# Zero-weight spare matmuls, a finer-grained head and a per-tile last layer norm in a two-layer attention kernel

## The chip, the cores and the metric

The kernel runs on one core of a Trainium2 chip. The metric is device time in microseconds (us). "The kernel before" is the tuned kernel that the change starts from, "the changed kernel" is the one after it. A run is called fast or slow by its state, and has the mean granted clock of the matrix engine beside it, where 1.0 is full speed. A single execution of this kernel varies with that clock by several us (the kernel before beside bz_late: 1630.98 us at 0.986, 1637.15 at 0.978), so every comparison below is made with several runs, and traces are compared by where in them a difference arises.

The engines: PE multiplies matrices (PEld is its weight load), ACT computes activation functions, DVE is the vector engine, POOL the general one, SP issues transfers.

## The reference

Two identical layers of attention and a GELU network on 2048 tokens of 512 values, with 32 heads of 16 values each:

```python
x = A_x                                                       # 1 x 2048 x 512, bf16
x = x + _A_ref(_layernorm(x), A_wqkv, A_wo)                   # attention, 32 heads
x = x + _B_ref(_layernorm(x), B_w1, B_b1, B_w2, B_b2)         # 512 -> 1792 -> 512, GELU
x = x + _A_ref(_layernorm(x), A_wqkv, A_wo)
x = x + _B_ref(_layernorm(x), B_w1, B_b1, B_w2, B_b2)
# _A_ref: softmax(q k^T / 4) v per head, then times wo
```

The softmax has 2 x 32 x 2048 x 2048 exponentials. They are cut into cells of 128 keys by 512 queries: 4096 cells, each one score matmul on PE.

## The kernel before

The program is laid out at build time by a scheduler that simulates the engines: generators yield operations with an estimated cost, a priority and the buffers that they read and write, and for each engine the scheduler picks the next one. Any edit that changes an operation's cost, priority or place can rearrange everything that comes after it.

Most cells go to ACT, as one instruction for one to three cells; the rest go to DVE, which makes an exponential with integer arithmetic in three steps.

```python
# ACT, in exps(): n cells of scores from PSUM to a buffer of probabilities
yield _Op("act", 0.065 + 0.4267 * n, lambda e, src=src, dst=dst: e.activation(
    out=dst, in_=src, func=ACT.Exp, scale=0.25), ...)
...
# DVE: dfirst() reads the scores, dchain() works on 16-bit integers in SBUF
yield _Op("dve", 0.68, lambda e: e.tensor_scalar(u, self.bank(b), E_SCALE, E_BIAS, op0=ALU.mult, op1=ALU.add), ...)
yield _Op("dve", 0.08 + 0.14 * n, lambda e: e.tensor_scalar(U[:, 1, 0:n, :], U[:, 0, 0:n, :], SHIFT, None, op0=ALU.add), ...)
yield _Op("dve", 0.08 + 0.28 * n, lambda e: e.tensor_scalar(U[:, 2:4, 0:n, :], U[:, 0:2, 0:n, :], 2 * SHIFT, None, op0=ALU.add), ...)
```

PE has less to do than ACT (in the trace before it is busy for 1430.3 us, ACT for 1560.7), and after it has idled its clock is at times halved (in the trace before, PE is busy for 0.12 us of the microsecond from 515 us, and the windows after it read 0.50). So the scheduler already puts spare matmuls, whose result nobody reads, into PE's gaps. They go into a PSUM bank that happens to be free, and only where the recent activity in its model is below a threshold:

```python
def fill(self, start, nxt):                       # before PE's next operation nxt, which can start at start
    while self.filler and self.mode:
        ...
        b, t = self.free(now, nxt.writes)         # a bank whose last result has been read
        now = max(now, t)
        if start - now < into + MM + back + FMARGIN or self.active(start) >= WARM:
            return
        op = self.filler(b, mode)                 # W2 times W2, one matmul of 128 columns or four of 32
```

The head: x comes in four transfers of 512 KB, the first tiles are normalized as a block of four, transposed on PE, and projected.

In the middle, once the first chunk's attention is through, POOL writes the ones column of the second layer's V:

```python
yield ("need", ("otn", 0, (0, 0, 512), 3))
yield _Op("pool", 1.0, lambda e: e.memset(T["V"][1][:, :, :, 16:17], 1.0), ...)
```

The tail, after the last exponential, is the output projection of attention (`wo`), a residual add, the last layer norm, the first GELU layer (`hpair`), GELU and the output tiles (`ytile`) of the last 256 tokens.

The softmax here doesn't subtract the row's maximum and nothing guards it: scores larger than these inputs give would overflow.

Of the kernel before, what the change touches and what calls it, by code (L numbers as in the profile page):

```python
# [15 lines left out]
F = 1792  # L16
# [38 lines left out]
WINDOW = 3.4  # L55
WARM = 0.38
FMARGIN = -0.1
FOLD = 0.1
DPRIO = 9
# [146 lines left out]
class _Sched:  # L206
# [5 lines left out]
    def __init__(self, P):  # L212
        self.P = P
        self.clock = {e: 0.0 for e in P.ENGS}
        self.end = {}
        self.pools = {}
        self.tokens = {}
        self.threads = []
        self.nseq = 0
        self.mode = None  # L220
        self.ops = []
        self.stream = []
        self.filler, self.free, self.fills = None, None, set()
# [86 lines left out]
    def fill(self, start, nxt):  # L310
        while self.filler and self.mode:
            now = self.clock["pe"]
            mode = "F" if nxt.mode == self.mode == "F" else "P"
            into, back = SW * (mode != self.mode), SW * (mode != nxt.mode) - SW * (nxt.mode != self.mode)
            b, t = self.free(now, nxt.writes)
            now = max(now, t)
            if start - now < into + MM + back + FMARGIN or self.active(start) >= WARM:
                return
            op = self.filler(b, mode)
            self.mode = mode  # L320
            ev = self.P.group("pe", op.fns, op.reads, op.writes)
            self.fills.add(ev)
            self.note(now + into, now + into + MM, op)
            self.ops.append(("pe", now, into + MM, "FILL"))
            self.clock["pe"] = now + into + MM
            self.end[ev] = self.clock["pe"] + LATENCY["pe"]
# [64 lines left out]
def bass_interleave_layers__mha_block__dense_activation_gelu__prompt_kernel(  # L391
# [15 lines left out]
    with ExitStack() as es:  # L407
# [39 lines left out]
        T["ONES1"] = sb([1, 128], BF16, "ones1")  # L447
        T["IDENT"] = sb([128, 128], BF16, "ident")
# [8 lines left out]
        sem_names = ["pe", "act", "dve", "pool", "dx0", "dx1", "dx2", "dx3", "dwq", "dwk", "dwv", "db1", "db2", "dw2",  # L457
# [37 lines left out]
class _Plan:  # L495
# [8 lines left out]
    def init(self):  # L504
        T, hbm = self.T, self.hbm

        def load(dst, src, sem, keys, cost):
            return _Op("sp", cost, lambda e: e.dma_start(dst, src), writes=keys, sem=sem, by=16, tail=2.0)

        yield _Op("pool", 0.1, lambda e: e.memset(T["IDENT"][:], 0.0), writes=["IDENT"])  # L510
        yield _Op("pool", 0.3, lambda e: e.affine_select(
            out=T["IDENT"][:], in_=T["IDENT"][:], compare_op=ALU.not_equal, fill=1.0, base=0, pattern=[[-1, 128]],
            channel_multiplier=1), reads=["IDENT"], writes=["IDENT"])
        yield _Op("pool", 0.1, lambda e: e.memset(T["NHALF"][:], -0.5), writes=["NHALF"])
        yield _Op("pool", 0.1, lambda e: e.memset(T["ONES1"][:], 1.0), writes=["ONES1"])
        yield _Op("dve", 0.6, lambda e: e.memset(self.bank(PVB), 0.0), writes=["B.%d" % PVB])
        yield _Op("dve", 0.1, lambda e: e.tensor_reduce(
            out=T["MASK"][:, :], in_=T["IDENT"][:, :].rearrange("p (a t d) -> p t a d", a=4, t=2, d=DH),
            axis=mybir.AxisListType.XY, op=ALU.add), reads=["IDENT"], writes=["MASK"])
        yield _Op("pool", 1.0, lambda e: e.memset(T["V"][0][:, :, :, 16:17], 1.0), writes=["V01"])  # L520
        yield ("need", ("otn", 0, (0, 0, 512), 3))
        yield _Op("pool", 1.0, lambda e: e.memset(T["V"][1][:, :, :, 16:17], 1.0),
                  writes=["V11"] + ["PART.0.%d" % g for g in range(8)])
        yield ("give", "v1ones")

    def loads(self):
# [13 lines left out]
        yield lx(0)  # L540
# [17 lines left out]
    def ln(self, tiles, dst, dkeys, prio, quick=False):  # L558
# [13 lines left out]
        yield _Op("pool", 1.0, lambda e: e.tensor_tensor(  # L572
# [8 lines left out]
    def ln_tile(self, c, t, dst, dkeys, quick):  # L581
# [16 lines left out]
        yield _Op("pe", 4 * TR, fns, reads=["XLN.%d" % x, "IDENT"], writes=["B.%d" % b])  # L598
        yield ("rel", "xln", x)
        t3 = tb[:, 0:512].rearrange("p (c q) -> p c q", c=NDC)  # L600
        if ph:
# [6 lines left out]
    def proj(self, l, kind, i, c, src, skeys, ph, done):  # L608
# [34 lines left out]
        if l:  # L643
            for r, j in zip(us, (0, 1) if kind == "V" else (i // 2,)):
                yield from self.wdone((l, (c, 0, 512), kind, j), r)
        cols = slice(512 * c, 512 * (c + 1))
# [9 lines left out]
        elif kind == "Q":  # L656
            yield _Op(ev, DV, lambda e: copy(e, T["Q"][:, i, cols], pb), reads=["B.%d" % b],
                      writes=["Q.%d.%d" % (i, c)])
        else:
            yield _Op("dve", DV, lambda e: e.tensor_copy(T["V"][l][:, i, :, 0:16], pb.rearrange("p (h d) -> p h d", h=H)),  # L660
                      reads=["B.%d" % b],
                      writes=["V%d.%d" % (l, i)] + (["PART.0.%d" % g for g in range(8)] if l else []))
        yield ("rel", "misc", b)
# [30 lines left out]
    def norm(self, l, seg, g, b, part, final):  # L694
# [8 lines left out]
        else:  # L703
            pt, pk = T["PART1"][:, g, :], "PART1.%d" % g
            over = ["K0.%d.%d" % (g // 2, c) for c in range(self.NQ)]
        if not final:
# [135 lines left out]
    def gelu(self, l, seg):  # L842
# [7 lines left out]
        fns = []  # L850
        for f in range(0, NFC, NFC // GP):
            g = T["G"][:, f:f + NFC // GP, seg[1]:seg[1] + n]
            if n == 512:
                g = g.rearrange("p a q -> p (a q)")
            fns.append(lambda e, g=g: e.activation(out=g, in_=g, func=ACT.Gelu_apprx_tanh))  # L855
        gk = self.gkeys(seg, range(NFC))
        yield _Op("act", GP * (0.065 + 0.4267 * NFC / GP * n / 512) + (2 - tail) * 1.28, fns, reads=gk, writes=gk, prio=2)
        for p in range(NFC // 2):
            yield ("give", ("g", l, seg, p))
# [26 lines left out]

    def post(self, l, seg):
# [5 lines left out]
        order = [(i, x) for i in range(NL) for x in self.segs[i]]  # L893
        prev = order[order.index((l, seg)) - 1] if (l, seg) != order[0] else None
# [4 lines left out]
        for t in tiles:  # L899
            yield ("need", ("xready", t, 2 * l + 1))  # L900
        self.phase[c] = 2 * l + 1
# [3 lines left out]
        yield ("spawn", self.ln(tiles, xf, xk, LNP, last), LNP)  # L905
# [31 lines left out]
    def first(self, c):  # L937
        T = self.T
        self.phase[c] = 0
        for t in range(4 * c, 4 * c + 4):  # L940
            yield ("give", ("xready", t, 0))
        yield from self.ln(range(4 * c, 4 * c + 4), lambda t: T["K"][1][:, :, t * 128:(t + 1) * 128], lambda t: ["XL.%d" % t],
                           5 + c, c == 0)
# [34 lines left out]
    def setup_attention(self):  # L978
# [22 lines left out]
        self.ended = False  # L1001
# [17 lines left out]
    def qpad(self):  # L1019
        T = self.T  # L1020
        for pi, (l, seg, g, kts, part, final) in enumerate(self.pas):
            b, ts = self.heads(seg, g)
# [10 lines left out]
    def free(self, now, ahead):  # L1033
        P = self.P
        best = (None, 1e9)
        for b in (6, 7, 0, 1, 2, 3, 4, 5) if "W2" in P.lastw else ():
            k = "B.%d" % b
            if k in ahead or not P.reads.get(k) and P.lastw.get(k) not in self.s.fills:
                continue
            t = max([0.0] + [self.s.end.get(ev, 0.0) + FOLD for ev in P.deps(["W2"], [k]) if ev[0] != "pe"])  # L1040
            if max(t, now) < max(best[1], now):
                best = (b, t)
        return best

    def filler(self, b, mode):
        T = self.T
        fns = []
        for a in range(1 if mode == "F" else 4):
            m = 128 if mode == "F" else 32
            o = self.bank(b)[m * a:m * a + m, :]  # L1050
            fns.append(lambda e, o=o, a=a, m=m: e.matmul(o, lhsT=T["W2"][:, 0, m * a:m * a + m], rhs=T["W2"][:, 1, :], start=True,  # L1051
                                                         stop=True, tile_position=(0, m * a)))
        return _Op("pe", MM, fns, reads=["W2"], writes=["B.%d" % b], mode=mode)
# [322 lines left out]
    def pvs(self):  # L1376
        T = self.T
        pools = self.s.pools
        for pi, (l, seg, g, kts, part, final) in enumerate(self.pas):
# [21 lines left out]
            def build(op, start, pi=pi, b=b, l=l, cols=cols, begun=begun, n=n):  # L1401
# [28 lines left out]
                op.cost = MM * rounds  # L1430

# [83 lines left out]
```

## Time and profile before

| kernel before | value |
|---|---|
| median of all its runs beside the changed kernel | 1632.34 us (1630.91 to 1634.13, 6 runs) |
| profiled span, mean clock | 1629.9 us, 0.986 |
| first exponential starts | 19.52 us |
| middle (first to last exponential) | 1581.28 us: ACT busy 1545.93, idle 35.35 |
| tail (from the last exponential) | 29.10 us |
| stretches at half clock in the middle | 11, together 44.4 us |

The lines themselves stand in the prediction below. They are read as a sum: head, ACT's work, ACT's idle, tail. A change can shorten the time only through one of these four.

### The profile page before, as it was taken

What the parts mean: (1) busy time and instruction counts of PE and PEld (TensorE: products, weight loads), DVE (VectorE), ACT (ScalarE), POOL (GpSimd) and SP (SyncE); (2) the same over time, 40 slices, a digit from 0 to 9 for tenths busy, and PEclk for the clock granted to TensorE, in tenths of its full rate; (3) what the DMA queues carried; (4) which work ended last, traced back from release to release, by engine and by line L of the source; (5) the groups of instructions that cost most, each with busy time, mean ns of one, the idle gap of its engine ahead of it and who ended that gap; (6) DMA issues with size and microseconds to landing.
All of it is one profiled execution on the core that took longest, in us unless ns stands there. A gap on an engine that the chain in (4) does not pass through costs nothing.

```text
span 1629.9 us, 32720 instructions
## 1 busy us (share of the span) xinstructions
PE 1430.3 (88%) x13701; PEld 418.1 (26%) x13838; DVE 1355.2 (83%) x2612; ACT 1560.7 (96%) x1402; POOL 111.6 (7%) x143
## 2 busy tenths in 40 slices
PE   6997888989898989899889989788898889888988
PEld 2222222222222222222222222222222222233434
DVE  6579999878887988987787788888888988897883
ACT  5999999999999999999998999989999999999995
POOL 3200000000000000000110001111000000000000
PEclk9999999999999999999999999999999999999999
DMA  5100001001010011100111001001101100010110
GB/s 173 22 1 1 1 14 34 27 4 39 25 33 27 1 27 40 34 27 1 27 46 47 7 14 40 2 1 27 46 11 30 34 14 11 17 40 24 50 53 27
DMA packets 88319, 44.85 MB, mean 28 GB/s; under 512 B 33645, under 2 KB 88174, under 8 KB 88174
## 3 DMA queue, kind: packets, MB, share of 16 engines
q1 hardware_dynamic: 88174, 42.75, 9.8%
q8 instruction: 111, 1.82, 0.5%
q14 instruction: 34, 0.28, 0.1%
HBM read 33.03 MB, written 2.10 MB: 22 GB/s over the span
## 4 chain that ended last, share of the span: by engine, by line
ACT 58%; PE 36%; DVE 3%; issue 1%; DMA 1%; POOL 0%; ACTq 0%
ACT pt L1360 49%; PE ps L1064 11%; PE ps L1421 11%; PE ps L868 4%; ACT v L1360 4%; PE ps L822 4%; PE ps L638 3%; ACT g L855 3%; ACT kt L1360 2%; PE ps L635 1%; DVE du L1209 1%; PE ps L749 1%; PE ps L1051 1%; ACT L855 1%; DMA xf<-xln 1%
## 5 line engine op out<-in xcount | busy, mean ns | idle before, releaser
L1360 ACT ACTIVATE pt<-ps 128x1024 bf16<-128x1024 f32 (+1 forms) x1217 | 1335.7, 1244 | 30.2 <-PE ps L1064 14.4
L1064 PE MATMUL ps<-qp,kt 32*128 32x512 bf16 x4096 | 545.5, 387 | 149.6 <-ACT pt L1360 109.5
L1209 DVE TENSOR_SCALAR du<-ps 128x512 uint16<-128x512 f32 x650 | 440.1, 685 | 112.7 <-PE ps L1064 106.2
L1421 PE MATMUL ps<-pt,v 128*17 128x512 bf16 (+1 forms) x3205 | 450.9, 364 | 2.3 <-ACT pt L1360 1.0
L1064 PEld LDWEIGHTS ps<-qp,kt 32*128 32x128 bf16 x4096 | 141.9, 91 | 700.6 <-ACT pt L1360 304.1
L1421 PE MATMUL ps<-du,vc 128*17 128x512 bf16 (+1 forms) x2178 | 305.1, 360 | 1.6 <-DVE du L1272 1.1
L1272 DVE TENSOR_SCALAR du<-du 128x2048 uint16<-128x2048 uint16 (+1 forms) x329 | 222.4, 681 | 2.5
L1028 POOL TENSOR_SCALAR qp<-q,mask 128x512 bf16<-128x512 bf16 (+1 forms) x92 | 68.7, 747 | 1273.0 <-PE ps L1064 1263.7
L1421 PE MATMUL ps<-du,v 128*17 128x512 bf16 (+1 forms) x726 | 140.3, 363 | 2.4 <-DVE du L1272 0.9
L1421 PEld LDWEIGHTS ps<-pt,v 128*17 128x17 bf16 x3205 | 107.6, 88 | 125.8 <-issue 96.7
L1270 DVE TENSOR_SCALAR du<-du 128x1024 uint16<-128x1024 uint16 (+1 forms) x329 | 136.6, 424 | 2.6
L868 PE MATMUL ps<-w,g 128*128 128x512 bf16 x404 | 118.5, 396 | 9.6 <-issue 5.7
L822 PE MATMUL ps<-xf,wr 128*128 128x512 bf16 (+1 forms) x427 | 111.0, 362 | 7.5 <-issue 5.6
L1360 ACT ACTIVATE v<-ps 128x1536 bf16<-128x1536 f32 (+1 forms) x77 | 102.6, 1354 | 4.0 <-PE ps L1421 2.0
L1421 PE MATMUL ps<-dh,vc 128*17 128x512 bf16 (+1 forms) x369 | 105.5, 360 | 0.1
L1421 PEld LDWEIGHTS ps<-du,vc 128*17 128x17 bf16 x2178 | 83.0, 89 | 58.5 <-issue 26.5
L836 DVE TENSOR_SCALAR g<-ps,hb1t 128x512 bf16<-128x512 f32 (+1 forms) x112 | 79.9, 713 | 16.8 <-PE ps L822 15.1
L1209 DVE TENSOR_SCALAR dh<-ps 128x512 uint16<-128x512 f32 x111 | 76.2, 686 | 12.1 <-PE ps L1064 9.2
L1209 DVE TENSOR_SCALAR kt<-ps 128x512 uint16<-128x512 f32 x98 | 67.3, 686 | 15.8 <-PE ps L1064 14.6
L1051 PE MATMUL ps<-w 128*32 128x512 bf16 x697 | 71.5, 398 | 1.8 <-DVE du L1209 1.6
L1360 ACT ACTIVATE kt<-ps 128x1536 bf16<-128x1536 f32 (+1 forms) x52 | 71.6, 1382 | 0.7 <-PE ps L1064 0.3
L1421 PE MATMUL ps<-kt,v 128*17 128x512 bf16 (+1 forms) x264 | 63.1, 365 | 0.1
(78 smaller groups left out, 1136.1 us busy)
## 6 DMA issues: line engine op xcount, KB each, us to landing
wr<-in_B_w_dram SPq DMA_DIRECT2D x59, 256.0 KB, 2.9
wr<-in_A_wqkv_dram SPq DMA_DIRECT2D x24, 256.0 KB, 2.8
wr<-in_A_wo_dram SPq DMA_DIRECT2D x18, 256.0 KB, 2.9
x<-in_A_x_dram SPq DMA_DIRECT2D x4, 512.0 KB, 8.5
out_dram<-x SPq DMA_DIRECT2D x16, 128.0 KB, 1.7
w<-in_B_w_dram SPq DMA_DIRECT2D x1, 1792.0 KB, 11.0
g<-in_A_wqkv_dram SPq DMA_DIRECT2D x3, 512.0 KB, 6.2
kt<-in_B_w_dram SPq DMA_DIRECT2D x4, 256.0 KB, 3.3
```

The costliest lines, as they stand in the source:

```text
L822: fns = [lambda e, dc=dc, j=j, pb=pb: e.matmul(pb, lhsT=T["WR"][w][:, 256 * dc + 128 * j:256 * dc + 128 * j + 128], rhs=T["XF"][:, dc, q], ...
L836: yield _Op("dve", 0.21 + n / 966, lambda e, fc=fc, pb=pb: e.tensor_scalar(T["G"][:, fc, q], pb, T["HB1T"][:, fc:fc + 1], None, op0=ALU.ad ...
L855: fns.append(lambda e, g=g: e.activation(out=g, in_=g, func=ACT.Gelu_apprx_tanh))
L868: fns = [lambda e, fc=fc: e.matmul(pb, lhsT=T["G"][:, fc, q], rhs=T["W2"][:, fc, :], start=(fc == 0), stop=False) for fc in range(NFC)]
L1028: yield _Op("pool", 0.1 + 0.6 * w / 512, lambda e, s=s, q=q, i=i, t=t, w=w: e.tensor_scalar(T["QP"][:, s, w * i:w * i + w], q, T["MASK"][: ...
L1051: fns.append(lambda e, o=o, a=a, m=m: e.matmul(o, lhsT=T["W2"][:, 0, m * a:m * a + m], rhs=T["W2"][:, 1, :], start=True, stop=True, tile_p ...
L1064: return (lambda e: e.matmul(o, lhsT=lhsT, rhs=rhs, start=True, stop=True, tile_position=(32 * a, 0)), ["K%d.%d.%d" % (l, gb, kt // 4), "Q ...
L1209: yield _Op("dve", 0.68, lambda e: e.tensor_scalar(u, self.bank(b), E_SCALE, E_BIAS, op0=ALU.mult, op1=ALU.add), reads=["B.%d" % b], write ...
L1270: yield _Op("dve", 0.08 + 0.14 * n, lambda e: e.tensor_scalar(U[:, 1, 0:n, :], U[:, 0, 0:n, :], SHIFT, None, op0=ALU.add), reads=key[0], w ...
L1272: yield _Op("dve", 0.08 + 0.28 * n, lambda e: e.tensor_scalar(U[:, 2:4, 0:n, :], U[:, 0:2, 0:n, :], 2 * SHIFT, None, op0=ALU.add), reads=k ...
L1360: yield _Op("act", 0.065 + 0.4267 * n, lambda e, src=src, dst=dst: e.activation(out=dst, in_=src, func=ACT.Exp, scale=0.25), reads=["B.%d" ...
L1421: op.fns.append(lambda e, o=o, lhsT=q[0][0][m], rhs=q[0][1][:, n * m:n * m + n], a=a, st=st, sp=sp: e.matmul(o, lhsT=lhsT, rhs=rhs, start= ...
```

## The change

Its intent has three parts. (1) Spare matmuls also where no bank is free: weights of zeros, added to a sum that is still open, in the output bank of attention (PVB). (2) A shorter head: x of the first chunk in four transfers with layer norm per tile, spare matmuls during the load to warm the clock, and the first Q multiplied from PSUM. (3) A finer tail: layer norm per tile, GELU released by halves, the copies on two engines. Cut to its core:

```diff
-WINDOW = 3.4
+WINDOW = 2.5
@@ free(): which bank a spare matmul may use
-        for b in (6, 7, 0, 1, 2, 3, 4, 5) if "W2" in P.lastw else ():
+        src = self.source()
+        for b in (6, 7, 0, 1, 2, 3, 4, 5) if src else ():
...
+        k = "B.%d" % PVB
+        if best[1] > now and self.pvopen and "W2" in P.lastw and k not in ahead:
+            best = (PVB, 0.0)
         return best
@@ filler()
+            start = b != PVB
+            if b == PVB:
+                w, o = T["ZERO"][:, 0:17], self.bank(b)[m * a:m * a + 17, :]
+            fns.append(lambda e, o=o, w=w, a=a, m=m: e.matmul(o, lhsT=w, rhs=rhs, start=start, stop=start, tile_position=(0, m * a)))
@@ loads(), first(): the head
-        yield lx(0)
+        for t in range(4):
+            yield load(T["X"][:, t, :], hbm["x"][:, t, :], "dxt%d" % t, ["X.%d" % t], 0.6)
...
+        for ts in (tiles,) if c else ([t] for t in tiles):
+            yield ("spawn", self.ln(ts, ..., 5 + c, c == 0), 5 + c)
@@ proj(): first Q from PSUM
+            yield _Op("dve", DV, lambda e: e.tensor_scalar(T["QP"][:, s, :], pb, T["MASK"][:, 0:1], None, op0=ALU.mult), ...)
@@ post(), ln_tile(): the tail
-        yield ("spawn", self.ln(tiles, xf, xk, LNP, last), LNP)
+        for ts in ([t] for t in tiles) if last else (tiles,):
+            yield ("spawn", self.ln(ts, xf, xk, LNP, last), LNP)
...
-        if ph:
+        if ph == 0 or t % 2 == 0:
             yield _Op("act", DV, lambda e: e.copy(dst(t), t3), ...)
```

## The prediction

> **What bounds the kernel now.** I read the page first. ACT is busy 96% of the span and heads the chain of work that ended last, and nearly all of its time is one line, the exponentials of the softmax (L1360).
>
> ```profile
> span 1629.9 us, 32720 instructions
> ...
> PE 1430.3 (88%) x13701; PEld 418.1 (26%) x13838; DVE 1355.2 (83%) x2612; ACT 1560.7 (96%) x1402; POOL 111.6 (7%) x143
> ...
> ACT 58%; PE 36%; DVE 3%; issue 1%; DMA 1%; POOL 0%; ACTq 0%
> ...
> L1360 ACT ACTIVATE pt<-ps 128x1024 bf16<-128x1024 f32 (+1 forms) x1217 | 1335.7, 1244 | 30.2 <-PE ps L1064 14.4
> ```
>
> So the time is ACT's work plus ACT's idle. The windows view, cut where the first exponential starts (19.52), where the last ends (1600.80) and where two tail stages begin, tells where the idle lies. After the window come its length and the busy time of PE, PEld, DVE, ACT and POOL, then clock, DMA share and GB/s.
>
> ```profile
> 0.00:15.45 15.45, 3.98 (x21) 2.27 (x22) 9.31 (x25) 1.29 (x2) 4.09 (x10) 1.00 0.93 293
> 15.45:19.52 4.07, 4.07 (x17) 1.28 (x15) 2.07 (x6) 1.65 (x4) 1.37 (x2) 1.00 1.10 348
> 19.52:1600.80 1581.28, 1399.02 (x13530) 402.09 (x13665) 1335.35 (x2565) 1545.93 (x1380) 105.43 (x130) 0.99 0.09 24
> 1600.80:1605.46 4.66, 2.68 (x14) 1.02 (x14) 3.12 (x8) 4.58 (x4) 0.00 (x0) 1.00 0.20 56
> 1605.46:1613.91 8.45, 7.51 (x38) 3.21 (x38) 3.97 (x11) 1.07 (x2) 0.71 (x1) 1.00 0.15 47
> 1613.91:1629.90 15.99, 13.02 (x85) 8.24 (x86) 1.38 (x2) 6.19 (x14) 0.00 (x0) 1.00 0.08 26
> ```
>
> Three parts: a head of 19.52 us before the first exponential, a middle of 1581.28 us in which ACT idles only 1581.28 - 1545.93 = 35.35 us, and a tail of 29.1 us that PE mostly fills. The waits of ACT in the middle are for PE: 14.4 us for scores (L1064) and 13.2 us for the probability-times-V matmuls (L1421) that give buffers back. One place of the idle is the clock: in eleven stretches, 44 us together ((1 - 0.986) of the span at half clock), windows of 1 us read 0.50. Here is one, just after a pair of GELUs:
>
> ```profile
> 515.00:516.00 1.00, 0.12 (x1) 0.00 (x0) 0.00 (x0) 0.99 (x2) 0.00 (x0) 0.82 0.00 0
> 516.00:517.00 1.00, 0.59 (x5) 0.15 (x5) 0.00 (x0) 1.00 (x2) 0.00 (x0) 0.50 0.00 0
> ...
> 518.00:519.00 1.00, 1.00 (x4) 0.19 (x2) 0.00 (x0) 0.62 (x1) 0.00 (x0) 0.50 0.00 0
> 519.00:520.00 1.00, 1.00 (x7) 0.20 (x6) 0.00 (x0) 0.04 (x1) 0.00 (x0) 0.50 0.00 0
> ```
>
> PE is nearly idle first, then fully busy at half clock, and ACT waits. Adding the ACT idle from one window before each slow stretch to five after it gives 11.7 us for the eleven (4.1 of them in one place, at 855 to 859 us, where ACT waits for buffers). The other 24 us of idle have full clock.
>
> [...]only 0.50 and 1.00 appear, and the first eight projections take 3.57 us (446 ns each) where four later ones take 1.03 (258). [...]GELUs of 3584 and 1792 columns differ by 3182 - 1688 = 1494 ns, 0.834 per column, and table loads take 1283. [...]256 KB weights land after 2.9 us. [...]
>
> **The change, part by part.** The instruction order of the built kernel gives counts; durations are the trace's.
>
> Head. Before, the whole first 512 KB of x is awaited, then four tiles are normalized as a block:
>
> ```profile
> 4.72 0.69 DVE L565 BATCH_NORM_STATS2 stats<-x 128x6 f32<-128x512 bf16 x1 [2.93 <-DMA x<-in_A_x_dram]
> ...
> 9.36 0.16 DVE L575 SCALAR_TENSOR_TENSOR nmr<-mv,rstd 128x4 f32<-128x4 f32 x1 [1.15 <-POOL rstd L572]
> ```
>
> After, tile 0 comes alone; 128 KB should land near 3.3 (an estimate: the moved bytes start near 2.7 us, at some 350 GB/s). DVE then runs its new order: statistics of tiles 0 and 1 to 5.0, the reciprocal root of one column on POOL about 0.55 (four columns took 1.03, two 0.71), the first two normalized tiles at 7.7 and 8.2, the last at 9.25. Four transposes (0.5 us) and an ACT copy (0.59) follow each, and two banks serialize them: the last copy ends near 10.7, against 13.5 for the first projection before. So 2.8 us there. Twelve spare matmuls run from 2 us on (identity as weights, ones as data). If they raise the clock, the K, Q and V projections take 3 x 0.9 instead of 3 x 1.75: up to 2.5 us more. They must, in the new order, all precede the first scores, as before. The first Q is multiplied from PSUM on DVE (0.69) rather than copied on ACT (0.59), then multiplied on POOL (0.69): 0.6 less, beside V's projection. First exponential near 14.2 if warm, 16.7 if not; I take 14.2 with some doubt: 5 us gained. The weights, at 350 GB/s, arrive by about 6.3, 7.8 and 9.3: just in time.
>
> Exponentials. A score cell (128x512) goes to ACT or, by integer arithmetic, to DVE. Counted by form, ACT has 3237 cells in 1346 instructions before, 3222 in 1337 after; DVE gets 15 more (874 against 859). With 0.427 us a cell, 1509.9 us of exponentials (groups L1360 over all outputs: 1335.7 + 102.6 + 71.6) leave (1509.9 - 1382) / 1346 = 0.095 us an instruction. ACT saves 15 x 0.427 + 9 x 0.095 = 7.3 us. DVE pays 15 x 1.24 = 19 us (685 ns to read the scores, and half of 426 + 688), at 83% busy beside ACT.
>
> Spare matmuls. Groups of four rise from 174 to 179, and 92 groups of zero weights into the open output bank are new; the window that the scheduler looks at shrinks from 3.4 to 2.5 us. At 0.21 us of pace each this is 20 us of PE's idle. Of the 11.7 us of idle around slow clock I expect half back: 6.
>
> Tail. GELU is released by halves, so half of the first output tile may start 1.65 us earlier; LN is per tile and the two copies go to ACT and DVE. But by the new order both statistics still follow both residual adds, and the second of these now waits until the first output tile is through. Walking it from the last exponential E: second residual add E + 8.2, statistics E + 9.5, POOL E + 11.1, both normalized E + 12.5, copies E + 13.2; before, the first matmul that reads them starts at 1613.91 - 1600.80 = 13.1. So nothing: I count 0.
>
> Sum: 1632.8 - 5 - 7.3 - 6 = 1614.5.
>
> **The rivals.** (a) Zero weights don't count as activity, or the spare matmuls don't raise the clock: head gains only 2.8 us, the middle only ACT's 7.3, and some idle returns: about 1623. For it: the spare matmuls already in before did not prevent the stretch at 515. (b) PE becomes the bound: it is 88% busy, and 92 more groups plus 45 more probability-times-V matmuls (three more per cell moved) delay scores; ACT waits eat the saved work: about 1630. Against it: they are put only into modelled gaps, and many groups of spares already ran with just 35 us of ACT idle. (c) It all works: the tail gains 2 us by PE's earlier start and the starvation at 855 us vanishes: 1604.
>
> **Range and chances.** A rearranged order moves small waits by some 5 us either way even with equal work. Adding that to the head's doubt (2.5) and the clock's (6) gives 1604 to 1626. More than 2% faster needs under 1600.1, that is 32.7 us: nearly all idle of the middle would have to go besides, so 0.05. Slower by 2% has nothing in the profile for it: 0.01.
>
> **What would show it.** Right: first exponential at 14 to 15; 3222 cells on ACT, busy 7 us less in L1360; mean clock above 0.99 with fewer 0.50 stretches after GELUs; ACT idle in the middle near 29; 29 us from last exponential to end. Wrong: projections of the head still at 430 ns; the same eleven slow stretches; PE waits of ACT above 35 us; a tail shorter than 28 us.

The sum stays 1632.8 - 5 - 7.3 - 6 = 1614.5. Its unit costs can be read from the trace before: 0.427 us a cell (ACT instructions of three cells take 1512 ns, of two 1084), 0.21 us of pace (three matmuls of 512 columns at 514.30 us take 0.81 us, one at 1604.48 takes 0.38), some 350 GB/s (347 to 378 in each microsecond from 3 to 8 us).

## More of the kernel before

In the first layer the units of later chunks are ordered K and V first, then Q, with priorities (smaller is sooner) 5 + c for chunk c and half a step more for Q:

```python
for j, (kind, i) in enumerate(units):
    p = prio + (0.01 * j if l else 0.5 if kind == "Q" and c > 0 else 0)
```

## The result, and the profile after

| | before | changed |
|---|---|---|
| median | 1632.34 us (6 runs) | 1620.86 us (1618.56 to 1621.65, 6 runs) |
| mean clock of the profiled run | 0.986 | 0.994 |

The ratio is 0.9928, with a 95% interval of 0.9915 to 0.9941. Ratios here are the mean time of one kernel's fast runs over that of the kernel before in the same rounds, so not quite the ratio of the medians. The time lies in the predicted range, and the change is within 2%.

First the page of the changed kernel: the span, the engines, the chain and the costliest group. In a group the number after the bar is busy time and mean ns of one, then the idle time in front of it and what ended most of that.

```profile
span 1619.2 us, 33814 instructions
...
PE 1459.1 (90%) x14297; PEld 421.7 (26%) x14297; DVE 1363.4 (84%) x2649; ACT 1554.1 (96%) x1396; POOL 111.7 (7%) x148
...
ACT 70%; PE 27%; DVE 2%; issue 1%; DMA 0%; POOL 0%; ACTq 0%; POOLq 0%
...
L1405 ACT ACTIVATE pt<-ps 128x1024 bf16<-128x1024 f32 (+1 forms) x1190 | 1308.5, 1255 | 30.9 <-PE ps L1466 14.8
```

ACT still bounds. Its waits in front of the exponentials have not shrunk (30.9 us here, 30.2 before), and the larger share of them is now for the probability-times-V matmuls (L1466), which give buffers back. The windows view, cut at the first and last exponential, gives the sum:

```profile
0.00:12.82 12.82, 9.64 (x45) 3.89 (x45) 6.78 (x24) 4.50 (x7) 5.87 (x15) 1.00 0.87 272
12.82:1589.76 1576.94, 1425.27 (x14100) 404.99 (x14099) 1347.85 (x2604) 1538.27 (x1372) 104.78 (x131) 0.99 0.10 26
1589.76:1619.20 29.44, 24.15 (x153) 12.82 (x153) 8.81 (x22) 11.34 (x18) 1.06 (x2) 0.98 0.12 36
```

ACT is busy for 1538.27 of the middle's 1576.94 us, so it idles 38.67. Against before: head -6.70, ACT's work -7.66, ACT's idle +3.32, tail +0.34, together -10.7. The idle has grown, although only 4 stretches at half clock are left in the middle (17.1 us; before 11 and 44.4), and the idle around them fell from 11.7 to 6.6 us. Idle elsewhere therefore rose from 23.7 to 32.1 us.

Where? The lead is by how much the changed kernel is ahead when the same score matmul, counted from the start, begins in both traces (worked out from its start in each):

| score matmul | 0 | 140 | 160 | 500 | 600 | 900 | 1400 | 2200 | last |
|---|---|---|---|---|---|---|---|---|---|
| lead over before, us | 6.6 | 6.5 | 2.0 | 2.3 | -2.0 | -3.7 | 0.7 | 8.3 | 11.3 |

The whole gain of the head is gone by score 600, handed back in two steps, with a third, smaller one before 900; the final 11 us come from later. The lead alone is not proof, as the two orders also place ACT's other work differently (at score 1800 it is -7.3, at 2300 it is 13.0). ACT's idle time, added up to the same scores, shows the same places: from 0.2 us less than before at score 140 it goes to 3.9 us more at 160, 4.5 at 500, 8.0 at 600 and 10.3 at 900; by 2600 it is down to 0.4, and at the end it is 3.3.

Step one, scores 140 to 160. The chain of waits of ACT between 76 and 90 us has one entry: engine and tile that waited, releaser, total, times, longest.

```profile
ACT pt L1405 <- PE ps L1109: 4.0, 1, 4.0
```

PE's timeline just before (start, duration, engine, line, operation, tiles, count) shows what it did instead of scores (L1109):

```profile
80.37 1.90 PE L647 MATMUL ps<-kt,g 128*128 128x512 bf16 x8
...
82.74 1.04 PE L647 MATMUL ps<-kt,g 128*128 128x512 bf16 x4
83.61 1.03 PE L644 MATMUL ps<-g,kt 128*128 128x512 bf16 x4
...
85.11 0.61 PE L1109 MATMUL ps<-qp,kt 32*128 32x512 bf16 x5
```

L647 makes K or Q, L644 makes V. The scores at 85.11 need K of the last chunk. In the order, eight Q matmuls of an earlier chunk stand ahead of that K, which is the priority rule shown above. ACT has run out of scores and waits.

Step two, scores 500 to 600. DVE and POOL in the timeline from 219.7 us:

```profile
219.70 2.51 POOL L530 MEMSET v<- 128x512 bf16 x1 [4.14 <-DVE xt L735]
219.87 0.24 DVE L740 RECIPROCAL rc<-xt 128x16 f32<-128x16 f32 x1
220.03 2.73 DVE L1317 TENSOR_SCALAR du<-du 128x2048 uint16<-128x2048 uint16 x1
```

The third line is the last DVE step of four cells, whose mean is 0.69 us over the run; here it takes 2.73 and ends 0.55 us after the memset. The reciprocal beside the memset is not delayed (0.24 us, the median of all 64 in this trace), the 16-bit operation is. That it is the memset that delays it is tested below by ones_split; why the one is delayed and the other not, no run shows. What follows is in a window of the stretch at half clock that comes next:

```profile
225.70:232.50 6.80, 6.71 (x36) 1.23 (x36) 4.17 (x9) 4.67 (x4) 0.00 (x0) 0.51 0.00 0
```

PE had stood still for 1.75 us up to 223.75, waiting for DVE, the clock fell for 6.8 us from 225.5, and now PE is busy throughout (6.71) at half speed while ACT has 4.67 of 6.80. In the kernel before the same memset blocks a DVE operation too (2.47 us at 222.6, where its mean is 0.43), but no slow stretch followed there.

Step three, in the waits of ACT between 330 and 342 us (total, times, longest):

```profile
ACT pt L1405 <- PE ps L1466: 4.8, 2, 2.9
```

In the kernel before there is one such wait, of 1.8 us. No experiment isolates this place. In return, a wait of 4.1 us of the kernel before at 855 us is 0.6 now.

The tail, from DVE's and PE's timeline around the layer norm (E, the last exponential's end, is 1589.76):

```profile
1597.41 0.68 DVE L777 TENSOR_TENSOR x<-x,ps 128x512 bf16<-128x512 bf16 x1
...
1603.27 3.22 PE L843 MATMUL ps<-xf,kt 128*128 128x256 bf16 x28 [0.39 <-DVE xf L613]
```

The second residual add starts at E + 7.65 and the first matmul behind the layer norm at E + 13.5 (predicted 13.2; before 13.1).

### The profile page after: what moved, and what is told of

Its sections match the earlier page's. It is cut to its first block, busy times and chain, and to the rows that moved or that the text cites. A ratio compares the mean times of both kernels' runs of the same rounds, so it can differ in the third digit from the quotient of the medians.

```text
span 1619.2 us, 33814 instructions
## 1 busy us (share of the span) xinstructions
PE 1459.1 (90%) x14297; PEld 421.7 (26%) x14297; DVE 1363.4 (84%) x2649; ACT 1554.1 (96%) x1396; POOL 111.7 (7%) x148
## 4 chain that ended last, share of the span: by engine, by line
ACT 70%; PE 27%; DVE 2%; issue 1%; DMA 0%; POOL 0%; ACTq 0%; POOLq 0%
ACT pt L1405 58%; PE ps L1466 8%; PE ps L1109 8%; ACT v L1405 5%; ACT kt L1405 4%; ACT g L878 3%; PE ps L889 3%; PE ps L843 2%; PE ps L647 2%; PE ps L644 1%; PE ps L770 1%; ACT L878 1%; ACT L1405 1%; PE ps L1097 1%; DVE du L1254 0%
## 5 line engine op out<-in xcount | busy, mean ns | idle before, releaser
L1405 ACT ACTIVATE pt<-ps 128x1024 bf16<-128x1024 f32 (+1 forms) x1190 | 1308.5, 1255 | 30.9 <-PE ps L1466 14.8
L1109 PE MATMUL ps<-qp,kt 32*128 32x512 bf16 x4096 | 539.4, 385 | 138.4 <-ACT pt L1405 92.8
L1254 DVE TENSOR_SCALAR du<-ps 128x512 uint16<-128x512 f32 x659 | 445.6, 686 | 114.9 <-PE ps L1109 106.8
L1466 PE MATMUL ps<-pt,v 128*17 128x512 bf16 (+1 forms) x3151 | 438.9, 362 | 5.1 <-ACT pt L1405 2.1
L1109 PEld LDWEIGHTS ps<-qp,kt 32*128 32x128 bf16 x4096 | 141.5, 91 | 687.7 <-ACT pt L1405 292.5
L1466 PE MATMUL ps<-du,vc 128*17 128x512 bf16 (+1 forms) x2211 | 308.6, 359 | 1.7 <-DVE du L1317 0.8
L1317 DVE TENSOR_SCALAR du<-du 128x2048 uint16<-128x2048 uint16 x332 | 227.9, 691 | 2.1
L1466 PE MATMUL ps<-du,v 128*17 128x512 bf16 (+1 forms) x737 | 141.2, 362 | 1.5 <-DVE du L1254 0.6
L1315 DVE TENSOR_SCALAR du<-du 128x1024 uint16<-128x1024 uint16 x332 | 135.3, 417 | 2.4
L1466 PEld LDWEIGHTS ps<-pt,v 128*17 128x17 bf16 x3151 | 105.7, 88 | 120.7 <-issue 86.7
L843 PE MATMUL ps<-xf,wr 128*128 128x512 bf16 (+1 forms) x472 | 123.8, 365 | 0.5 <-DVE g L857 0.2
L1466 PE MATMUL ps<-dh,vc 128*17 128x512 bf16 (+1 forms) x384 | 108.6, 359 | 0.0
L1466 PEld LDWEIGHTS ps<-du,vc 128*17 128x17 bf16 x2211 | 85.0, 89 | 58.9 <-issue 28.4
L1405 ACT ACTIVATE kt<-ps 128x1536 bf16<-128x1536 f32 (+1 forms) x66 | 93.3, 1420 | 2.3 <-PE ps L1466 1.4
L857 DVE TENSOR_SCALAR g<-ps,hb1t 128x512 bf16<-128x512 f32 (+1 forms) x112 | 79.9, 713 | 12.3 <-PE ps L843 10.9
L1466 PE MATMUL ps<-kt,v 128*17 128x512 bf16 (+1 forms) x311 | 77.2, 365 | 0.0
## 6 DMA issues: line engine op xcount, KB each, us to landing
w<-in_B_w_dram SPq DMA_DIRECT2D x1, 1792.0 KB, 10.9
```

What stands on the lines that cost most here:

```text
L843: fns = [lambda e, dc=dc, j=j, pb=pb: e.matmul(pb, lhsT=T["WR"][w][:, 256 * dc + 128 * j:256 * dc + 128 * j + 128], rhs=T["XF"][:, dc, q], ...
L857: yield _Op("dve", 0.21 + n / 966, lambda e, fc=fc, pb=pb: e.tensor_scalar(T["G"][:, fc, q], pb, T["HB1T"][:, fc:fc + 1], None, op0=ALU.ad ...
L1109: return (lambda e: e.matmul(o, lhsT=lhsT, rhs=rhs, start=True, stop=True, tile_position=(32 * a, 0)), ["K%d.%d.%d" % (l, gb, kt // 4), "Q ...
L1466: op.fns.append(lambda e, o=o, lhsT=q[0][0][m], rhs=q[0][1][:, n * m:n * m + n], a=a, st=st, sp=sp: e.matmul(o, lhsT=lhsT, rhs=rhs, start= ...
```

## The experiments

Twelve kernels ran, in four series of three rounds, each series beside the kernel before on one chip. The series ran on three chips, so across series the ratios compare better than the medians. Unless told otherwise an edit is made in the changed kernel. Each has 4 runs, and all outputs were correct, also with zeros added to an open sum. The table collects the terms of most of the profiled runs; the text then takes the runs one by one. "Slow" is the number of stretches at half clock in the middle and their length.

| run | ratio | first exp. | ACT busy | ACT idle | tail | slow |
|---|---|---|---|---|---|---|
| kernel before | 1 | 19.52 | 1545.93 | 35.35 | 29.10 | 11: 44.4 |
| changed kernel | 0.9928 | 12.82 | 1538.27 | 38.67 | 29.44 | 4: 17.1 |
| zero_narrow | 0.9985 | 12.74 | 1540.01 | 44.99 | 29.42 | 11: 54.6 |
| before_zero | 0.9933 | 19.95 | 1543.25 | 28.07 | 29.03 | 3: 13.7 |
| x_one | 0.9950 | 14.49 | 1546.79 | 32.12 | 29.40 | 3: 20.5 |
| ones_split | 0.9905 | 12.36 | 1538.06 | 34.72 | 29.43 | 3: 10.2 |
| q_late | 0.9886 | 12.41 | 1542.15 | 28.91 | 29.43 | 2: 10.2 |
| bz_late | 0.9901 | 19.20 | 1541.69 | 27.15 | 29.06 | 3: 17.1 |
| wo_first | 0.9897 | 12.46 | 1538.18 | 36.08 | 27.19 | 4: 13.7 |
| os_wo | 0.9878 | 12.65 | 1537.52 | 33.63 | 27.19 | 1: 3.4 |
| best1 | 0.9889 | 12.47 | 1542.15 | 29.68 | 27.20 | 1: 10.2 |

### Which spare matmuls matter

**zero_narrow.** The order stays, but the zero-weight spares stream one column instead of 512:

```diff
-            fns.append(lambda e, o=o, w=w, a=a, m=m: e.matmul(o, lhsT=w, rhs=rhs, start=start, ...
+            fns.append(lambda e, o=o, w=w, k=1 if b == PVB else 512, a=a, m=m: e.matmul(o[:, 0:k], lhsT=w, rhs=rhs[:, 0:k], start=start, ...
```

> The changed kernel, every instruction in the same place, but the 368 zero-weight spare matmuls are one column long instead of 512, so PE has next to nothing to do in them. Theory (zero weights count as activity for the clock): the slow-clock stretches come back, mean clock falls from 0.994 to about 0.988, and the time rises by 3 to 6 us. Rival (zero weights are worth nothing to the clock; the better clock of the changed kernel comes from where the other spares stand): clock stays 0.993 to 0.996 and the time stays within 1.5 us.

Measured: 1631.66 us (1628.99 to 1636.63), ratio 0.9985 (0.9965 to 1.0005), clocks 0.973 to 0.983. The group of the narrowed spares, and then the windows view of the middle:

```profile
L1097 PE MATMUL ps<-w,zero 128*17 128x1 bf16 x368 | 14.6, 169 | 0.0
```

```profile
12.74:1597.74 1585.00, 1420.08 (x14100) 405.41 (x14099) 1348.16 (x2604) 1540.01 (x1372) 104.90 (x131) 0.98 0.10 25
```

PE has less to do, the other instructions and their order are the same, and the kernel is slower than the changed one, by 10.8 us in the medians and 9.3 in the ratios, more than the 3 to 6 expected (the profiled run is the fastest of the four). The zero-weight spares hold the clock (0.991 to 0.996 in the changed kernel, where they are whole), and that is worth far more than the idle right beside slow stretches suggested.

**all_narrow.** All spares after the head, with zero weights and with real ones, stream one column; the twelve in the head stay whole.

```diff
+            fns.append(lambda ..., k=1 if src == ["W2"] else 512, ...: e.matmul(o[:, 0:k], lhsT=w, rhs=rhs[:, 0:k], ...
```

> The changed kernel in the same order, with all spare matmuls after the head (zero-weight and weighted, 1087) one column long; the twelve in the head stay whole. Theory (spares hold the clock and are otherwise harmless): clock falls well below that of the kernel before, to 0.96 or less, and the time rises by 10 us or more. Rival (spares take PE time that the scores need, so they cost about what they save): the clock falls but the time stays within 4 us.

Measured: 1652.61 us (1643.65 to 1662.16), ratio 1.0111 (1.0067 to 1.0154), clocks 0.937 to 0.954. With next to nothing to do in these spares, the changed kernel is slower than the kernel before, which has its own at full length.

**all_zero.** The groups of four spares that go into free banks get zero weights too; the order stays.

```diff
+            fns.append(lambda ..., w=T["ZERO"][:, 0:32] if src == ["W2"] and m == 32 and b != PVB else w, ...
```

> The changed kernel, same order on every engine, but the groups of four spare matmuls that had real weights (179 groups, into free banks) get zero weights as well, 32 columns each. Theory: what holds the clock is that the array is streamed through, not what stands in it: mean clock 0.993 to 0.996 and the ratio 0.991 to 0.994, as with real weights. Rival: zero weights count for less than real ones: then the clock falls below 0.985 (with spares of one column it was 0.946) and the ratio rises above 0.998.

Measured: 1619.87 us (1619.15 to 1622.59), ratio 0.9917 (0.9890 to 0.9944), clocks 0.993 to 0.995. Zero weights serve as well as real ones (1620.86 us, clocks 0.991 to 0.996), within the noise. The rival falls.

**before_zero.** The kernel before with part (1) alone: the zero-weight spares in PVB and the shorter window.

```diff
-WINDOW = 3.4
+WINDOW = 2.5
@@ free(), filler(): as in the change, with W2 as the only source
```

> The kernel before with one part of the change alone: spare matmuls with zero weights into the open output bank and the shorter window of the scheduler (222 groups of four with real weights instead of 174, and 69 with zeros). ACT's work is nearly the same (3235 cells in 1348 instructions; before 3237 in 1346), head and tail are as before. Theory: this part alone raises the mean clock from about 0.98 to 0.99 or more and gives what its loss cost in the changed kernel (10.8 us): ratio 0.992 to 0.995. Rival: the clock is raised but PE, with more to do, or other waits hand it back: clock 0.99 or more and ratio 0.998 to 1.001.

Measured: 1622.02 us (1619.77 to 1622.18), ratio 0.9933 (0.9912 to 0.9954), clocks 0.996 and 0.997. The spares in its trace, with real weights and with zeros, and then its windows:

```profile
L1062 PE MATMUL ps<-w 128*32 128x512 bf16 x889 | 82.5, 385 | 1.6 <-DVE du L1219 1.3 <-DVE kt L1219 0.3
L1062 PE MATMUL ps<-w,zero 128*17 128x512 bf16 x276 | 26.6, 382 | 0.0
```

```profile
0.00:19.95 19.95, 8.15 (x37) 3.60 (x37) 11.39 (x30) 2.93 (x4) 5.51 (x13) 1.00 0.96 303
19.95:1591.27 1571.32, 1435.92 (x14131) 409.45 (x14130) 1336.16 (x2569) 1543.25 (x1382) 107.21 (x130) 1.00 0.09 24
1591.27:1620.30 29.03, 23.40 (x145) 12.46 (x145) 8.46 (x19) 11.83 (x20) 0.71 (x1) 1.00 0.12 37
```

The counts are those expected: 222 groups with real weights instead of 174, and 69 with zeros. So part (1) acts in two ways here, and this run does not separate the zeros from the shorter window and the 48 more ordinary groups that came with them. In the changed kernel the groups with real weights rise only from 174 to 179, and there zero_narrow does separate the zeros.

This is the main finding. Part (1) by itself brings what the whole change brings, 0.9933 against 0.9928. The middle is 10 us shorter than before (1571.32 against 1581.28), and 5.6 us shorter than that of the whole change (1576.94). So what the whole change has beyond it, parts (2) and (3) and the order that they bring, starts 7.1 us earlier and saves 5.0 us more of ACT's work, and loses nearly all of it in 10.6 us more of idle. The lead of the changed kernel over this one shows where: 7.0 us at score 0, 6.9 at 140, 2.4 at 160, 2.6 at 500, -1.7 at 600, -1.1 at 800, -4.6 at 900. These are the three places seen above. ACT's idle, added up to the same scores, is 3.9 us more than here at 160, 7.9 at 600 and 11.3 at 900; after that it falls to 3.5 more at 2600 and rises to 10.6 at the end, so the later part also gains and loses in turn.

### What the head is worth

**warm_narrow.** The twelve spare matmuls of the head stream one column.

```diff
+            fns.append(lambda ..., k=1 if src != ["W2"] else 512, ...: e.matmul(o[:, 0:k], lhsT=w, rhs=rhs[:, 0:k], ...
```

> The changed kernel in the same order, with the twelve spares of the head one column long. The first projections should take about 3.5 us for eight as in the kernel before instead of 1.9, and the first exponential should move from 12.8 to 15 to 16 us. Theory (the 4.0 us wait of ACT at 81 to 85 us is set by the projections of the last chunk, which do not hang on the first exponential): that wait shrinks by about what the head loses and the whole time rises by less than 1.5 us. Rival (the wait follows the head along): it stays at 4 us and the time rises by 2.5 us or more.

Measured: 1621.45 us (1619.61 to 1622.61), ratio 0.9918 (0.9903 to 0.9933). Its PE timeline in the head, and then its one entry in the waits of ACT between 78 and 95 us:

```profile
9.63 3.57 PE L647 MATMUL ps<-kt,g 128*128 128x512 bf16 x8 [0.77 <-ACT kt L611]
...
14.85 0.84 PE L1109 MATMUL ps<-qp,kt 32*128 32x512 bf16 x5
```

```profile
ACT pt L1405 <- PE ps L1109: 4.0, 1, 4.0
```

Without the spares eight projections take 3.57 us instead of 1.89, and the first exponential starts at 15.50 instead of 12.82. So the spares do speed up the projections. I read this as the clock, by their durations: four matmuls of 512 columns take 1.89 us in a stretch at 0.50 (trace before, 517.49 us), four projections at 1.00 take 1.04 (changed kernel, 82.74 us). The clock column is no evidence this early: in warm_narrow it reads 1.00 between 9.6 and 13.2 us, while those eight projections take 446 ns each. My reason for expecting the loss to vanish (the wait at 81 us would shrink) fell: the wait has moved along and is as long as before. Nevertheless the time is the same. In the profiled run the 2.6 us are regained at scores 540 to 560 (1.7) and 600 to 620 (0.8), where the slow stretches are 3.4 and 0 us long instead of 6.8 and 3.4. The clocks of its four runs, 0.994 to 0.998, lie a little above those of the changed kernel, 0.991 to 0.996. Why they do, and so why the time is the same, is not settled.

**x_one.** The first 512 KB of x in one transfer again; the rest of the head stays.

```diff
-        for t in range(4):
-            yield load(T["X"][:, t, :], hbm["x"][:, t, :], "dxt%d" % t, ["X.%d" % t], 0.6)
+        yield load(T["X"][:, 0:4, :], hbm["x"][:, 0:4, :], "dxt0", ["X.%d" % t for t in range(4)], 2.5)
```

> The changed kernel, but the first 512 KB of x come in one transfer again (layer norm still per tile, spares of the head and first Q from PSUM kept). Theory: the first tile is used at 4.7 instead of 2.9 us, and the first exponential moves from 12.8 to about 14.6. Its order after the head is another one (3245 cells in 1343 instructions on ACT instead of 3222 in 1337), which by my count of the prediction would cost 23 x 0.427 + 6 x 0.095 = 10.4 us more; the version with Q later has shown that such a count overstates it (there ACT was busy 4.1 us longer where the count said 6.5, and it idled 10 us less). So I expect 1.8 us for the head and 4 to 8 for the cells, less what its waits differ: ratio 0.994 to 0.999. Rival: the head's gain is handed back in the first chunks, as with cold projections: ratio 0.992 to 0.994.

Measured: 1625.06 us (1621.91 to 1625.64), ratio 0.9950 (0.9924 to 0.9977). The four transfers are worth 1.7 us at the first exponential (14.49 against 12.82), as expected. The order after it differs: ACT is busy 8.5 us more and idles 6.6 us less. Between these two orders, most of the work that the scheduler moved from ACT to DVE came back as idle of ACT; as work and order changed together, it is not shown that the one made the other. The ratio lies within the expected band, but at the end of it where little of the cells' cost is left, and its interval still overlaps the rival's.

### Mending the hand-backs

**q_late.** Q of later chunks goes behind K of the chunks that follow.

```diff
-            p = prio + (0.01 * j if l else 0.5 if kind == "Q" and c > 0 else 0)
+            p = prio + (0.01 * j if l else 4 if kind == "Q" and c > 0 else 0)
```

> The changed kernel with one edit: in the first layer, Q of the later chunks gets a later place in the order than K of the chunks that follow. Theory: the wait of ACT at 81 to 85 us (4.0 us, for scores that need K of the last chunk) is due to eight Q matmuls ahead of that K, so it shrinks to about 1. But the order of everything after changes with it, and this kernel gives ACT 12 cells and 14 instructions more: 12 x 0.427 + 14 x 0.095 = 6.5 us. Net about 3 us slower than the changed kernel: ratio 0.994 to 0.996. Rival 1: the split of cells costs nothing, because ACT idles elsewhere anyway: ratio 0.990 to 0.991. Rival 2: the wait stays at 4 because it is set by the layer norms, not by Q: then ratio 0.997.

Measured: 1614.56 us (1613.84 to 1618.08), ratio 0.9886 (0.9859 to 0.9913). My theory fell, though not in its first half: ACT has no wait at all between 72 and 90 us. It has 12 cells more and is busy 3.9 us longer, but rival 1 holds: idle falls by 9.8 us. Besides the wait for K, the waits near 225 and 335 us are gone. The memset is still there, but the 16-bit DVE operation now starts ahead of it. DVE's timeline, then POOL's:

```profile
216.05 0.65 DVE L1317 TENSOR_SCALAR du<-du 128x2048 uint16<-128x2048 uint16 x1
216.62 0.24 DVE L740 RECIPROCAL rc<-xt 128x16 f32<-128x16 f32 x1
```

```profile
216.18 2.76 POOL L530 MEMSET v<- 128x512 bf16 x1 [4.19 <-DVE xt L735]
```

Here POOL comes second, its memset takes 2.76 us instead of 2.51 (a small difference, on an engine whose times are rough in the profile), and DVE works on.

**ones_split.** The memset in eight pieces; the order on PE, DVE and ACT is exactly that of the changed kernel.

```diff
-        yield _Op("pool", 1.0, lambda e: e.memset(T["V"][1][:, :, :, 16:17], 1.0), ...)
+        for k in range(0, self.NT, 2):
+            yield _Op("pool", 0.3, lambda e, k=k: e.memset(T["V"][1][:, k:k + 2, :, 16:17], 1.0), ...)
```

> The changed kernel with one edit: the memset on POOL that writes the ones into the second layer's V (one instruction, 2.51 us at 219.7 in its trace) becomes eight of two tiles each. The order on PE, DVE and ACT is the same. Theory: that memset blocks the DVE operation beside it (2.73 us instead of 0.68), PE then starves, the clock falls at 225.7 for 6.8 us, and ACT waits about 3.5 us there. So: no DVE operation of 2.7 us near 220, no slow stretch at 225, lead regained 2 to 3.5 us by score 600, mean clock 0.996 or more, ratio to the kernel before 0.9905 to 0.992 (the changed kernel had 0.9928 in its own rounds). Rival: the idle of ACT there is slack that is only passed on to the next wait: the ratio stays at 0.993, with the DVE operation short all the same.

Measured: 1617.75 us (1616.35 to 1619.78), ratio 0.9905 (0.9874 to 0.9936), clocks 0.993 to 0.997. The same place in its timeline, and then the window that follows it:

```profile
219.24 4.02 POOL L531 MEMSET v<- 128x64 bf16 x8 [4.14 <-DVE xt L735]
219.57 0.78 DVE L1317 TENSOR_SCALAR du<-du 128x2048 uint16<-128x2048 uint16 x1
```

```profile
226.00:233.00 7.00, 6.84 (x66) 1.87 (x65) 6.48 (x14) 6.67 (x7) 0.00 (x0) 1.00 0.01 2
```

The DVE operation takes 0.78 us, the clock stays at 1.00 and ACT is busy 6.67 of 7 us. The lead over the changed kernel is 0.5 us up to score 500, 4.3 at 560, 5.2 at 700 and 4.6 at the end: the gain is made at this place, and it is kept. It is more than the 2 to 3.5 us expected. With nothing else moved, this is the cleanest of the experiments, but 4 us is the upper end of what the memset costs. The kernel wo_first (below) has the same memset and the same order up to the tail, and its DVE operation is blocked as well:

```profile
219.66 2.71 DVE L1317 TENSOR_SCALAR du<-du 128x2048 uint16<-128x2048 uint16 x1
```

Yet the stretch at half clock behind it is 3.4 us long instead of 6.8, and there the splitting (os_wo against wo_first) is worth 2.0 us at score 600. So one memset of 2.5 us, on an engine that is 7% busy, cost 2 to 4 us, by how the clock fell. In the times alone the gain is not clear of noise: the median is 3.1 us lower, but the interval overlaps that of the changed kernel (0.9915 to 0.9941).

**bz_late.** The control: before_zero with the same edit as q_late, so with the old head.

```diff
-            p = prio + (0.01 * j if l else 0.5 if kind == "Q" and c > 0 else 0)
+            p = prio + (0.01 * j if l else 4 if kind == "Q" and c > 0 else 0)
```

> A control: the kernel before with the zero-weight spares alone (0.9933) and Q of the later chunks later as well, so that the only large parts missing of the Q-later version (0.9886) are the new head and the per-tile tail. ACT gets 3230 cells in 1349 instructions (3235 in 1348 without the edit; 3234 in 1351 with the new head). Theory: with the old head ACT reaches the first chunks late enough that the Q matmuls cost it nothing there (the wait near 96 us was 1.6), so the edit alone gives little: ratio 0.991 to 0.994, first exponential near 19.9, and the 7.5 us of the new head are what separates it from 0.9886. Rival: the edit gains by itself in the old head too, and the new head is worth nothing even with its waits mended: ratio 0.987 to 0.990.

Measured: 1618.04 us (1616.91 to 1619.07), ratio 0.9901 (0.9879 to 0.9923): just between the two theories. Against before_zero the gain is not in the first chunks (lead 0.8 us at score 0, 0.0 at 600) but later (3.8 at 900, 8.1 at 2600, 3.2 at the end), so it is another order's luck more than the wait for K. Against q_late the question of the head is answered better: q_late leads by 6.6 us at score 0 and still by 7.2 at score 900, and by 4.1 at the end, 3.5 by the medians, which are from different series and chips; the intervals of the two ratios overlap. So with its waits mended the new head seems to be worth about 4 of its 7 us; the rest goes in the later part, where the two orders differ, and I can't tell apart there what is due to the head.

### The tail

**wo_first.** In the last chunk the output projections of attention get priority over the output tiles.

```diff
-                      writes=["B.%d" % b], prio=MID if h else FPRIO)
+                      writes=["B.%d" % b], prio=1.0 if (l, seg) == (NL - 1, self.segs[l][-1]) else MID if h else FPRIO)
```

> The changed kernel with one number changed: the output projections of the last half segment go ahead of the first output tiles in PE's order. If the tail gained nothing because the second residual add waited behind the first output tile (as the prediction walked it), the first matmul on the last normalized tiles starts about E + 11.3 instead of E + 13.5 (E the last exponential's end), and the tail is 27 us instead of 29.4, the time 2 to 2.5 us less. Rival (PE's work alone sets the tail): the tail stays within 0.7 us.

Measured: 1617.59 us (1614.26 to 1619.57), ratio 0.9897 (0.9877 to 0.9917). Its last exponential ends at 1586.72; DVE's and PE's timeline:

```profile
1590.86 1.28 DVE L777 TENSOR_TENSOR x<-x,ps 128x512 bf16<-128x512 bf16 x2 [1.20 <-PE ps L770]
...
1597.98 3.23 PE L843 MATMUL ps<-xf,kt 128*128 128x256 bf16 x28
```

Both residual adds are done by E + 5.4 instead of E + 8.3, the layer norm's result is multiplied at E + 11.3, and the tail is 27.19 us instead of 29.44. The order ahead of the tail is the same; that its last exponential also ended 3 us sooner in this run I put down to the clock (the slow stretch near 225 us is 3.4 us long instead of 6.8). So the per-tile layer norm had something to gain; it lacked the early second residual add.

### Together

**os_wo.** ones_split and wo_first in one kernel: the two diffs, cut to their new lines.

```diff
+            yield _Op("pool", 0.3, lambda e, k=k: e.memset(T["V"][1][:, k:k + 2, :, 16:17], 1.0), ...)
+                      writes=["B.%d" % b], prio=1.0 if (l, seg) == (NL - 1, self.segs[l][-1]) else MID if h else FPRIO)
```

> The changed kernel with two edits that touch different stages: the memset of ones in eight pieces, and in the last chunk the output projections of attention ahead of the output tiles (measured alone: tail 27.2 instead of 29.4 us, ratio 0.9897). Theory: the two add up: ratio 0.9870 to 0.9890, last exponential some 2 to 3 us earlier than in the changed kernel and the tail at 27 us. Rival (the memset's gain is only passed on): ratio 0.9895 to 0.991, last exponential at 1587 to 1590.

Measured: 1613.82 us (1612.77 to 1615.47), ratio 0.9878 (0.9852 to 0.9904), clocks 0.996 to 0.999. The two add up, as expected (0.9870 to 0.9890). The last exponential ends 6.0 us earlier than in the changed kernel, more than the 2 to 3 expected; one stretch at half clock, of 3.4 us, is left in the middle.

**best1.** q_late, ones_split and wo_first: those two lines, and this one.

```diff
+            p = prio + (0.01 * j if l else 4 if kind == "Q" and c > 0 else 0)
```

> The changed kernel with all three edits that helped alone: Q of later chunks after K of later chunks (0.9886), ones of V in eight small memsets (0.9905), output projections of the last chunk first (0.9897). Theory: Q later has already moved the memset away from the operation that it blocked (no idle at scores 540 to 560 in its trace), so only the tail adds: 2.2 us off 0.9886, ratio 0.987 to 0.988. Rival: all three add up: 0.9885 - 0.0022 - 0.0014 = 0.985 or below.

Measured: 1614.09 us (1613.30 to 1615.59), ratio 0.9889 (0.9868 to 0.9909). Its tail is 27.2 us, but 0.9889 is no better than q_late alone (0.9886), and it misses the 0.987 to 0.988 that I expected: the splitting of the memset adds nothing, as expected, and the 2.2 us of the tail don't show beyond the runs' spread; in the profiled run a slow stretch of 10.2 us lies near 1312 us where q_late had one of 6.8. The medians are 1614.09 and 1614.56, from different series. os_wo and best1 both beat both kernels (neither interval overlaps that of the changed kernel, 0.9915 to 0.9941), and can't be told apart from each other.

## Why the prediction was right or wrong

The total was right, 1614.5 in a range of 1604 to 1626 against 1620.86, and so was the class. The sum behind it was not: two of its terms were mis-sized in opposite directions, and one assumption was wrong. That the total still fell into the range is partly luck: 10.3 us more idle than before had gathered by score 900, and 7 of them were made good later, by waits of the kernel before that the new order does not have.

- **Head, predicted -5.** Right in mechanism and a little small: -6.7. The first tile was used at 2.88 us (predicted 3.3), the last transposed copy ended at 9.49 (10.7), and the projections ran warm (eight in 1.89 us), about which I had doubted; warm_narrow shows 2.7 us for that and x_one 1.7 us for the four transfers.
- **Exponentials, predicted -7.3.** ACT's work fell by 7.66 us. As a term of the time it was wrong: compared with before_zero, ACT does 5.0 us less and idles 10.6 more, and x_one and q_late do more work and idle less. I had charged the moved cells to DVE as free because DVE was 83% busy; an average of that kind did not tell whether the moved cells come out as waits.
- **Spare matmuls, predicted -6.** The step took half of the idle in the neighbourhood of slow stretches, and that idle did fall by 5.1. But the worth of the spares was mis-sized: part (1) brings 10.9 us alone (0.0067 of 1633; there with 48 more ordinary groups besides the zeros), and losing the zeros costs the changed kernel 9 to 11. A slow stretch seems to cost more than the idle within 5 us of it: its waits would surface later, when buffers that it delayed are missing. The waits for L1466 in particular, far from any half clock, are rarer in before_zero (8.3 us in its main group; 13.2 before). That this is the path is my reading of these groups, not shown by itself.
- **The assumption that other waits stay, so that idle ends near 29.** This is the step that failed. Idle ended at 38.67 us. The head's gain was handed back at three places: Q ahead of K (4.0 us), the memset that blocks DVE (2 to 4 us, shown by ones_split and os_wo), and the buffers at 333 to 340 us (3 us more than before; not isolated). My range allowed "some 5 us either way" for rearranged order; away from slow stretches it was 8.4 us net, towards more idle.
- **Tail, predicted 0.** Right: +0.34, and for the reason given, the second residual add, as wo_first shows by moving it. Rival (c)'s tail gain of 2 us is there once that add is early. Its other half happened: of the wait at 855 us 0.6 us is left.
- **Rival (a), zero weights don't count as activity.** Refuted by zero_narrow (clocks 0.973 to 0.983 instead of 0.991 to 0.996) and all_zero (0.993 to 0.995), and for the spares of the head, whose weights are not zero, by warm_narrow.
- **Rival (b), PE becomes the bound.** Not as put: before_zero's PE is busy 1467 us (91%), more than the changed kernel's 1459, and its ACT idles 10.6 us less. But in the first chunks, where Q stands ahead of K, PE's order does bound for 4 us.
- **Slips in the working.** The 44 us at half clock are about twice (1 - 0.986) of the span, not once. Rival (c), with the two gains that it names, gives 1614.5 - 2 - 4.1 = 1608.4, not 1604. And the doubts named for the range add up to 13.5 us either way, so 1601 to 1628. None of them changes what came out right or wrong.

## What to carry to other kernels

An earlier start is a loan until the next wait: follow the lead of the changed kernel over the old one along a count of equal work, together with the idle of the bounding engine, and the places where the one falls and the other grows name what to mend. Where PE's clock falls after it has idled, as it did here (0.12 us busy in one microsecond, then 0.50), spare matmuls with zero weights into an open sum need no free bank; here these and the shorter window, without the rest of the change, brought the whole gain (0.9933 against 0.9928). Before counting work moved off the bounding engine as time saved, run a version with the same order and one part undone: a rearranged schedule changes waits by as much as the parts are worth.
